# Causal dilated convolution with a gate: first loads in other pieces, a fixed order of issue, and another order of units

## The chip, the cores and the metric

One core of one Trainium2 chip runs the kernel; the arrays lie in the chip's memory before and after. The metric is device time in microseconds (us) of one execution, and the time of a kernel is the median of its runs. The profile is of one execution, recorded by the hardware profiler, and has its own time.

The engines carry the profile's names: PE (TensorE, matmuls), PEld (its weight loads), DVE (VectorE), ACT (ScalarE), POOL (GpSimd) and SP (SyncE, which here issues DMAs only). Each engine works through its own instructions in the order in which they are written down; a semaphore holds an instruction, and all behind it on that engine, until what it needs is done.

## The reference

The input x is 2 x 16000 x 144 (batch, time, channels), the taps w are 15 x 144 x 288, and w_o is 144 x 144, all bf16. Each output row is a causal convolution with dilation 2, a gate and a projection:

```python
dil = 2
pad = (K - 1) * dil
xp = jnp.pad(x, ((0, 0), (pad, 0), (0, 0)))
h = jnp.einsum('btc,cd->btd', xp[:, pad:pad + T, :], w[0])
for i in range(1, K):
    off = pad - i * dil
    h = h + jnp.einsum('btc,cd->btd', xp[:, off:off + T, :], w[i])
f = h[..., :D].copy()
g = h[..., D:].copy()
z = jnp.tanh(f) * _sigmoid(g)
return z @ w_o
```

with D = 144 and K = 15.

## The kernel before

**Layout.** The 32,000 rows are cut into 128 stretches of 250, one for each partition, so one tile is one time step of all stretches: 128 rows by 144 channels. To use time steps as the matmul's stationary operand, each tile is transposed. The 144 channels are split into 128 (tiles XA, multiplied by the taps WA) and 16 (eight steps of 16 channels packed into 128 rows: tiles XB, taps WB). A matmul multiplies a 128x128 tile by 128x288 taps into a PSUM bank of 288 columns: 144 for f, 144 for g. Time is counted in octets of eight tiles; there are 31, and 28 tiles of history precede them.

**The first ten rows and the rest.** The first ten time steps are computed straight, with 15 taps each for the 128 channels and two matmuls for the 16 (`direct`, L1096, `direct_b`, `direct_all`, L1127). The rest goes through a fast scheme that needs fewer matmuls: DVE forms differences of transposed tiles (V, DU, DD, BD, and over pairs of octets GX, GU, GV, GD, lines L724 to L810) and sums of taps (WC, WS, WT, WV, WD, `wsum`, L659). Two octets make a pair and each pair two units, one for its even and one for its odd steps; there are 30 units.

**A unit.** Its steps are named in a string, `ORDER` (L18), which is walked once for each unit; steps that take a bank to the next unit's partial sums act one unit ahead. XC and XR make the part with DU and GU (taps WT and WS, WB with XB), CV and CD the part with XA, V and DD (WT, WV, WD), SR the part with GX (WC), EF the part with GV and the four accumulations by DVE (L1061), DD the last part with GD and BD. UP is POOL's addition (L997), PJ a projection (L918) with its eviction by ACT (L922). Copies of a bank into another (`copy`, L960) and evictions to UC, UD and XS (`evict`, L475 as one piece for adjacent banks, L478 as two) are ACT's. The last part of a unit is evicted by ACT as sigmoid and tanh into TG, and DVE multiplies them into Z (L841). Z is transposed by DMA (ZT) and projected.

**The planner.** `_Graph` holds all operations with their reads and writes. `schedule` runs a simulated list scheduling, ten passes, with costs from the `dur` numbers written at each operation and due times of the pass before, and the best pass gives each engine's order and the PSUM banks. PE may take operations up to `PE_WIN` (L17) places ahead of the program's order; other engines go by due time. The parameter `soft` of `add` makes an operation start after others in the plan without a semaphore on the chip; before the change no operation uses it. `assign` gives each kind of DMA a ring of semaphores, and a load whose turn in the ring falls on a semaphore in use waits until the earlier load has landed.

**The start.** PE first runs 40 warm-up matmuls (`warm`, L583) on constants. The first 38 tiles of x (28 of history, 2 that the octets leave over, and octet 0) come in four pieces (`pro_pieces`: 14, 8, 8 and 8 tiles). Each of the first three comes in two loads, of 112 and of 15 partitions; partition 0 of all three comes by two small loads on ACT's queue, and its place in the history is zeroed later. The taps come in four (`wa_pieces`: 10 to 14, 6 to 9, 2 to 5, 0 and 1). SP issues them in the planner's order: x, x, x, x, WA, WA, x, x, WA, x, WA, then WB (L559), then the first chunks of Xr (`load_xchunk`, L665), the x for later octets, each of 16 tiles. The taps use three semaphores, and the fourth waits for the first one; every chunk of Xr carries a dependence on the load of taps 0 and 1 (`wa_op`), and so do the 16 loads of w_o on POOL's queue. The 15-row piece of the first x load, like the others, is issued by SP.

`transposes` (L600) transposes a piece's tiles by PE (L612) into a PSUM bank that ACT or DVE evicts into XA (L618), and DVE zeroes the columns that lie across the two batches (L625) once for each octet. `compact_pro` packs the last 16 channels (L577), and `b_halo` (L631) zeroes part of that on POOL, has PE transpose it (L647) and ACT evict it to XB (L650). The banks 6 and 7 serve these transposes besides 5, and bank 6 the warm-up (`BANK_O`). Six banks, 0 to 5, hold the first six rows. Then, for each piece of taps, six groups of matmuls (`direct`) run, and the transposes of the next piece stand ahead of the six. Two matmuls (L1119) then clear banks 6 and 7.

**Later octets.** ACT copies the first four octets of Xr to STA (L684) and DVE the later ones; SP transposes STA into XA by DMA (L689). For the 16 channels DVE makes C from Xr (L675), SP transposes T from C (L711), stores T to memory and loads it back (s<-T, XB<-s, L701), and copies part of the last octet's XB (XB<-XB, L701).

## Time and profile before

| | |
|---|---|
| median of the runs | 313.43 us (3 runs, 313.32 to 313.61) |
| the profiled execution | 314.19 us, of which the span is 312.6 us |
| instructions | 7564, of them 2586 matmuls |
| busy share of the span | PE 97%, DVE 93%, ACT 83%, PEld 76%, POOL 32% |
| granted clock of TensorE | full speed in all 40 slices |
| moved by DMA | 48.47 MB, mean 155 GB/s |

The span runs from the first to the last recorded instruction; the execution's own time holds what lies around it as well. Times in the views are us from the start of the span, and durations are of one group of like instructions, in which the end of one may overlap the start of the next. L816 is the line of `region` and `mm`, where most matmuls are recorded, so they are told apart by their tiles.

### The profile page before, as it was taken

The page shows a single profiled execution, that of the slowest core. Times are in us where ns is not written, and L with a number is a line of the kernel's source. Part 1 is how long each engine was busy: PE and PEld are TensorE (multiplying, and loading weights), DVE is VectorE, ACT ScalarE, POOL GpSimd, SP SyncE. Part 2 cuts the span into 40 slices and gives each one's busy share as a digit, 9 for nine tenths or more (in the row PEclk, how much of TensorE's full clock was granted, in tenths as well). Part 3 has the DMA queues.
Part 4 walks back from the last instruction along what each step waited for, and adds up shares of the span by engine and source line. Part 5 has one row for each costly group of instructions (what it writes and reads, how often), then busy time and mean ns, then how long its engine had stood idle before and what let it go on. Part 6 is the DMA issues. An engine that isn't in the chain of part 4 may idle for free.

```text
span 312.6 us, 7564 instructions
## 1 busy us (share of the span) xinstructions
PE 303.5 (97%) x2586; PEld 237.9 (76%) x2586; DVE 291.6 (93%) x651; ACT 258.7 (83%) x835; POOL 99.9 (32%) x89
## 2 busy tenths in 40 slices
PE   7989998999999999999999999999999999999995
PEld 7867675677787878787777778777787877778784
DVE  1899699999999999999999999999999999999764
ACT  3365697788998888899888888998888899888894
POOL 7920142333222333332133333222333332233330
PEclk9999999999999999999999999999999999999999
DMA  7964755859667485856749686674759586461342
GB/s 209 302 110 133 168 138 140 126 159 135 197 154 184 137 177 163 173 168 151 186 130 173 165 173 189 138 203 116 160 164 209 159 116 147 120 142 52 103 115 113
DMA packets 100067, 48.47 MB, mean 155 GB/s; under 512 B 88222, under 2 KB 90719, under 8 KB 100029
## 3 DMA queue, kind: packets, MB, share of 16 engines
q1 hardware_dynamic: 99513, 47.66, 63.3%
q0 software_dynamic: 512, 0.33, 0.5%
q8 instruction: 20, 0.33, 0.5%
q14 instruction: 18, 0.15, 0.1%
q10 hardware_dynamic: 4, 0.01, 0.0%
HBM read 13.77 MB, written 10.20 MB: 77 GB/s over the span
## 4 chain that ended last, share of the span: by engine, by line
PE 89%; DMA 4%; ACT 2%; DVE 2%; SPq 1%; issue 1%; ACTq 0%
PE PS L816 79%; PE PS L918 9%; DMA Xr<-in_x_dram 2%; DMA WA<-in_w_dram 2%; DVE DD L724 1%; ACT PS L960 1%; ACT STA L684 1%; SPq L517 1%; SPq L559 1%; ACT TG L478 1%; PE PS L878 0%; PE PS L940 0%; DVE Xp L987 0%; ACT XA L618 0%; ACT TG L475 0%
## 5 line engine op out<-in xcount | busy, mean ns | idle before, releaser
L997 POOL TENSOR_TENSOR UX<-UC,XS 128x576 f32<-128x576 f32 x60 | 84.3, 1425 | 201.2 <-ACT UC L475 95.5
L816 PE MATMUL PS<-WA,GD 128*128 128x288 bf16 x450 | 87.3, 286 | 1.2 <-DVE PS L1061 1.2
L960 ACT ACTIVATE PS<-PS 128x288 f32<-128x288 f32 x210 | 81.4, 443 | 0.5 <-PE PS L816 0.4
L816 PE MATMUL PS<-WB,BD 128*128 128x288 bf16 x240 | 67.5, 286 | 0.0
L475 ACT ACTIVATE TG<-PS 128x288 bf16<-128x288 f32 x130 | 47.6, 438 | 16.8 <-PE PS L816 16.7
L478 ACT ACTIVATE TG<-PS 128x144 bf16<-128x144 f32 x240 | 50.7, 315 | 8.7 <-PE PS L816 8.6
L816 PEld LDWEIGHTS PS<-WA,GD 128*128 128x128 bf16 x450 | 42.5, 98 | 14.5 <-DVE PS L1061 2.5
L922 ACT ACTIVATE OS<-PS 128x432 bf16<-128x432 f32 (+1 forms) x88 | 43.1, 490 | 12.4 <-PE PS L918 11.9
L1061 DVE TENSOR_TENSOR PS<-PS,Xp 128x288 f32<-128x288 f32 x120 | 49.5, 458 | 1.5 <-PE PS L816 0.5
L1061 DVE TENSOR_TENSOR PS<-PS,UX 128x288 f32<-128x288 f32 x120 | 49.3, 456 | 0.0
L987 DVE TENSOR_TENSOR Xp<-PS,UD 128x576 f32<-128x576 f32 x60 | 42.7, 751 | 3.6 <-ACT UD L478 3.4
L816 PE MATMUL PS<-WS,GU 128*128 128x288 bf16 x210 | 45.0, 286 | 0.4 <-ACT PS L960 0.4
L918 PE MATMUL PS<-WOR,ZT 128*128 128x144 bf16 (+1 forms) x322 | 43.3, 253 | 0.0
L816 PE MATMUL PS<-WC,GV 128*128 128x288 bf16 x210 | 37.7, 287 | 0.5 <-ACT PS L960 0.5
L816 PE MATMUL PS<-WB,XB 128*128 128x288 bf16 x140 | 37.6, 286 | 0.0
L918 PEld LDWEIGHTS PS<-WOR,ZT 128*128 128x128 bf16 x322 | 28.4, 98 | 5.8
L841 DVE TENSOR_TENSOR Z<-TG 128x576 bf16<-128x576 bf16 (+1 forms) x63 | 27.7, 440 | 3.7 <-ACT TG L475 3.6
L816 PE MATMUL PS<-WD,DD 128*128 128x288 bf16 x210 | 30.7, 286 | 0.0
L816 PEld LDWEIGHTS PS<-WB,BD 128*128 128x128 bf16 x240 | 23.5, 98 | 5.9
L816 PEld LDWEIGHTS PS<-WS,GU 128*128 128x128 bf16 x210 | 20.4, 98 | 6.6 <-ACT PS L960 1.3
L816 PEld LDWEIGHTS PS<-WD,DD 128*128 128x128 bf16 x210 | 19.5, 98 | 6.7 <-ACT PS L960 1.7
L816 PE MATMUL PS<-WT,DU 128*128 128x288 bf16 x120 | 24.5, 286 | 0.1
(87 smaller groups left out, 475.0 us busy)
## 6 DMA issues: line engine op xcount, KB each, us to landing
out_dram<-OS SPq DMA_DIRECT2D x31, 288.0 KB, 2.3
Xr<-in_x_dram SPq DMA_DIRECT2D x15, 576.0 KB, 4.6
XB<-XB SPq DMA_DIRECT2D x30, 192.0 KB, 3.2
XB<-s SPq DMA_DIRECT2D x59, 32.0 KB, 2.0
s<-T SPq DMA_DIRECT2D x30, 32.0 KB, 3.5
WA<-in_w_dram SPq DMA_DIRECT2D x2, 288.0 KB, 5.4
ZT<-Z SPq DMA_TRANSPOSE x32, 3.0
Xp<-in_x_dram SPq DMA_DIRECT2D x2, 252.0 KB, 4.9
```

Source lines behind the costliest of these rows:

```text
L475: return e.activation(bass.AP(t[:].tensor, off + (0 if st > 0 else n), [[row, NP], [st, 2], [1, n]]), bass.AP(PS[:].tensor, lo * 512 + c0, ...
L478: ins = e.activation(bass.AP(t[:].tensor, off + i * n, [[row, NP], [1, n]]), bass.AP(PS[:].tensor, q.phys * 512 + c0, [[8 * 512, NP], [1, ...
L517: return e.dma_start(tile_ap, src)
L559: return e.dma_start(WB[0:n * DB, par, :], src)
L816: return lambda t: t.matmul(bank(b), lhsT=lhs(), rhs=rhs(), start=start, stop=True, skip_group_check=True)
L841: g.add("dve", lambda v: v.tensor_tensor(dst(), TG[:, s, 1, 2 * k:2 * k + n, :], TG[:, s, 0, 2 * k:2 * k + n, :], ALU.mult), r=[("TG", s, ...
L918: return t.matmul(PS[:, c0:c0 + n * D], lhsT=ZT[:, zt, blk_, :], rhs=WOR[:, wi_:wi_ + n, :].rearrange("p a b -> p (a b)"), start=first, st ...
L922: g.add("act", lambda e: e.activation(OS[:, os_, a:c, :].rearrange("p e d -> p (e d)"), PS[:, bo.phys * 512:bo.phys * 512 + (c - a) * D], ...
L960: g.add("act", lambda e: e.activation(bank(c), bank(b), ACT.Copy), r=[("bank", b)], w=[("bank", c)], dur=0.29, prio=prio)
L987: return v.tensor_tensor(ue(u % NU, q, 0, 2).rearrange("p (v n) -> p v n", v=2), src, UD[:, u % NUD, :, :], ALU.add)
L997: op = g.add("pool", lambda p: p.tensor_tensor(UX[:, u % NU, h, :, :], UC[:, 0, :, :], bass.AP(XS[:].tensor, h * N2, [[2 * N2, NP], [0, 2] ...
L1061: g.add("dve", lambda e, dst=dst, src=src, ua=ua: e.tensor_tensor(bank(dst), bank(src), ua(), ALU.add), r=[("bank", src), ("UX", us, h) if ...
```

## The change

What it does, part by part:

- The first loads come in five pieces of x (10, 4, 8, 8, 8 tiles) and five of taps (13 and 14, 10 to 12, 6 to 9, 2 to 5, 0 and 1), issued by SP in turn: a piece of x, then a piece of taps. A chain of `soft` links (`first`) fixes this order in the plan, on SP and on ACT. The 15-row load of the first x piece moves to ACT's queue, with the halo rows, ahead of ACT's first activation.
- Semaphores: five for the taps instead of three, twelve for x instead of eight. WB and the first two Xr chunks are linked behind the taps by `soft` alone, and the dependence of chunks on taps 0 and 1 is gone. The loads of w_o keep theirs, and those taps are now issued last.
- The transposes: in the plan 50 warm-up matmuls (40 and 10) stand ahead of the first piece's transposes instead of 40, and the 12 behind them are gone; the transposes of the next piece stand between the second and the third group of `direct` of a piece; `b_halo` stands between the fourth and fifth group of the fourth piece. Octet -3, which two banks hold, is transposed, evicted and zeroed by halves, and taps wait for the half that they read (`xa_key`).
- The warm-up writes bank 4 instead of 6 (`BANK_O`).
- `ORDER` and `PE_WIN` change, and with them the plan of all engines: in the string DD00 moves behind CV, CD0, XC0 and CD1, XR0 ahead of SR0, SR1 ahead of DD11 and DD10, and UP0 and UP1 to the end.

```diff
-PE_WIN = 28
-ORDER = "EF0 PJ EF1 XC1 DD00 CV CD0 XC0 CD1 XR1 DD11 UP0 SR0 XR0 DD01 DD10 PJ UP1 SR1 PJ"
+PE_WIN = 26
+ORDER = "EF0 PJ EF1 XC1 CV CD0 XC0 CD1 DD00 XR1 XR0 SR0 PJ DD01 SR1 PJ DD11 DD10 UP0 UP1"
...
-    BANK_O = 6
+    BANK_O = 4
...
-        wa_pieces = [(10, 15), (6, 10), (2, 6), (0, 2)]
...
-        pro_pieces = [(0, 14), (14, 22), (22, E0), (E0, EP)]
...
+        chain = {"sp": None, "act": None}
+
+        def first(eng, fn, key, dur, dma, nbytes):
+            op = g.add(eng, fn, w=key, dur=dur, dma=dma, nbytes=nbytes, soft=(chain[eng],))
+            chain[eng] = op
+            return op
+
+        def halo(key, e0, n):
+            first("act", lambda e: e.dma_start(flat(Xp[0:1, e0:e0 + n, :]), bass.AP(x_t, 0, [[L * D, 1], [1, n * D]])), [key], 0.5, "xp", n * 288)
         for pi, (e0, e1) in enumerate(pro_pieces):
-            if pi:
...
-                g.add("sp", ld_w(t0, t1), w=[("WA", pi - 1)], dur=0.55, dma="wa", nbytes=(t1 - t0) * 128 * N2 * 2)
             if e0 >= H:
-                g.add("sp", ld_x(flat(Xp[:, e0:e1, :]), 0, NP, e0, e1), w=[("Xp", pi, 0), ("Xp", pi, 1)], dur=0.45, dma="xp", nbytes=NP * (e1 - e0) * D * 2)
-                continue
-            g.add("sp", ld_x(flat(Xp[1:1 + n16, e0:e1, :]), 1, 1 + n16, e0, e1), w=[("Xp", pi, 0)], dur=0.45, dma="xp", nbytes=n16 * (e1 - e0) * D * 2)
-            g.add("sp", ld_x(flat(Xp[1 + n16:NP, e0:e1, :]), 1 + n16, NP, e0, e1), w=[("Xp", pi, 1)], dur=0.45, dma="xp", nbytes=15 * (e1 - e0) * D * 2)
-        g.add("act", lambda e: e.dma_start(flat(Xp[0:1, 0:H, :]), bass.AP(x_t, 0, [[L * D, 1], [1, H * D]])), w=[("Xp", 0, 2)], dur=0.5, dma="xp", nbytes=8064)
-        g.add("act", lambda e: e.dma_start(flat(Xp[0:1, H:E0, :]), bass.AP(x_t, 0, [[L * D, 1], [1, KD * D]])), w=[("Xp", 2, 2)], dur=0.5, dma="xp", nbytes=576)
...
-        wa_op = g.add("sp", ld_w(t0, t1), w=[("WA", 3)], dur=0.55, dma="wa", nbytes=(t1 - t0) * 128 * N2 * 2)
...
+                first("sp", ld_x(flat(Xp[:, e0:e1, :]), 0, NP, e0, e1), [("Xp", pi, 0), ("Xp", pi, 1)], 0.45, "xp", NP * (e1 - e0) * D * 2)
+            else:
+                first("sp", ld_x(flat(Xp[1:1 + n16, e0:e1, :]), 1, 1 + n16, e0, e1), [("Xp", pi, 0)], 0.45, "xp", n16 * (e1 - e0) * D * 2)
+                first("act" if pi == 0 else "sp", ld_x(flat(Xp[1 + n16:NP, e0:e1, :]), 1 + n16, NP, e0, e1), [("Xp", pi, 1)], 0.45, "xp", 15 * (e1 - e0) * D * 2)
+                if pi == 0:
+                    halo(("Xp", 0, 2), 0, H)
+                    halo(("Xp", 3, 2), H, KD)
+            t0, t1 = wa_pieces[pi]
+            wa_op = first("sp", ld_w(t0, t1), [("WA", pi)], 0.5, "wa", (t1 - t0) * 128 * N2 * 2)
+        xp_keys = [[("Xp", pi, 0), ("Xp", pi, 1)] + ([("Xp", 0, 2)] if pi < 4 else []) + ([("Xp", 3, 2)] if pi == 3 else []) for pi in range(5)]
...
+        g.add("act", lambda a: a.activation(SCR[:, 0:32], SCR[:, 32:64], ACT.Sigmoid), r=["SCR"], w=["SCR2"], dur=1.5, soft=(chain["act"],))
...
-        g.add("sp", ld_wb(0), w=[("WB", 0)], dur=0.5, dma="wb", nbytes=73728)
-        g.add("sp", ld_wb(1), w=[("WB", 1)], dur=0.5, dma="wb", nbytes=64512)
+        first("sp", ld_wb(0), [("WB", 0)], 0.5, "wb", 73728)
+        first("sp", ld_wb(1), [("WB", 1)], 0.5, "wb", 64512)
...
             for o in range(-4, 1):
-                es = [e for e in range(max(0, E0 + 8 * o), E0 + 8 * o + 8)]
-                if not (e0 <= es[0] < e1):
-                    continue
                 for h, (j0, j1) in enumerate(XA_PARTS[o]):
                     eng, b = XA_ENG[o][h]
+                    es = [E0 + 8 * o + j for j in range(j0, j1)]
+                    if not e0 <= es[0] < e1:
+                        continue
                     fns = []
                     for e in es:
                         i = oct_of(e)[1]
-                        if j0 <= i < j1:
-                            fns.append((lambda e_, b_, i_: (lambda t: t.transpose(PSb[:, b_ * 1024 + 128 * i_:b_ * 1024 + 128 * i_ + 128], Xp[:, e_, 0:DA], ID[:])))(e, b, i))
+                        fns.append((lambda e_, b_, i_: (lambda t: t.transpose(PSb[:, b_ * 1024 + 128 * i_:b_ * 1024 + 128 * i_ + 128], Xp[:, e_, 0:DA], ID[:])))(e, b, i))
...
-                    g.add(eng, ev, r=[("bank", HB[b])], w=[("XA", aslot(o), h)] if o < 0 else [("XA", aslot(o))], dur=(0.08 + 0.115 * (j1 - j0)) if eng == "act" else (0.05 + 0.08 * (j1 - j0)))
-                z0 = 2 if o == -4 else 0
-                z1 = 6 if o == -1 else 8
-                if o < 0:
-                    def zc(v, o_=o, i0_=z0, i1_=z1):
-                        dst = XA[:, aslot(o_), i0_:i1_, :].rearrange("p s (b q) -> p s b q", q=SEG)[:, :, :, 0]
-                        return v.memset(dst, 0.0)
-                    g.add("dve", zc, r=[("XA", aslot(o), h) for h in range(len(XA_PARTS[o]))], w=[("XA", aslot(o))], dur=0.08)
+                    last = h == len(XA_PARTS[o]) - 1
+                    key = ("XA", aslot(o)) if last else ("XA", aslot(o), h)
+                    g.add(eng, ev, r=[("bank", HB[b])], w=[key], dur=(0.08 + 0.115 * (j1 - j0)) if eng == "act" else (0.05 + 0.08 * (j1 - j0)))
+                    z1 = min(j1, 6) if o == -1 else j1
+                    if o < 0 and j0 < z1:
+                        def zc(v, o_=o, i0_=j0, i1_=z1):
+                            dst = XA[:, aslot(o_), i0_:i1_, :].rearrange("p s (b q) -> p s b q", q=SEG)[:, :, :, 0]
+                            return v.memset(dst, 0.0)
+                        g.add("dve", zc, r=[("XA", aslot(o), q) for q in range(h)] if last else [], w=[key], dur=0.08)
...
-            return g.add("sp", ld_x(flat(Xr[:, s, 0:c - a, :]), 0, NP, E0 + a, E0 + c), w=[("Xr", s)], dur=0.5, dma="xr", nbytes=NP * (c - a) * D * 2)
+            return g.add("sp", ld_x(flat(Xr[:, s, 0:c - a, :]), 0, NP, E0 + a, E0 + c), w=[("Xr", s)], dur=0.5, dma="xr", nbytes=NP * (c - a) * D * 2, soft=(chain["sp"],) if ci < 2 else ())
...
+        def xa_key(e):
+            o, i = oct_of(e)
+            return ("XA", aslot(o), 0) if o == -3 and i < XA_PARTS[o][0][1] else ("XA", aslot(o))
...
-                  r=[("XA", aslot(o)) for o in sorted(set(oct_of(e - DIL * i)[0] for i in range(t0, t1)))] + [("WA", pi)], w=[("bank", b)], dur=(t1 - t0) * MM)
+                  r=sorted(set(xa_key(e - DIL * i) for i in range(t0, t1))) + [("WA", pi)], w=[("bank", b)], dur=(t1 - t0) * MM)
...
-        load_xchunk(0).deps.add(wa_op)
+        load_xchunk(0)
+        transposes(0)
+        warm(10)
         for pi, (t0, t1) in enumerate(wa_pieces):
-            if pi == 0:
-                transposes(0)
-                warm(12)
-            if pi < 3:
-                transposes(pi + 1)
-            if pi == 2:
-                b_halo()
             for k in range(6):
+                if k == 2 and pi < 4:
+                    transposes(pi + 1)
+                if k == 4 and pi == 3:
+                    b_halo()
                 direct(k, HB[k], pi, t0, t1)
...
-                load_xchunk(nl[0]).deps.add(wa_op)
+                load_xchunk(nl[0])
...
-        g.assign(mksem, {"xp": 8, "wa": 3, "wb": 2, "xr": NX, "xa": 4, "xb": 10, "zt": 3, "st": 4, "wor": 16})
+        g.assign(mksem, {"xp": 12, "wa": 5, "wb": 2, "xr": NX, "xa": 4, "xb": 10, "zt": 3, "st": 4, "wor": 16})
```

17 lines of the change are left out of this document (7 added, 10 removed).

## The prediction

> **What bounds the kernel now.** I read the page first, then the busy time by stretches, then the order of time where an engine idles.
>
> ```profile
> span 312.6 us, 7564 instructions
> ...
> PE 89%; DMA 4%; ACT 2%; DVE 2%; SPq 1%; issue 1%; ACTq 0%
> ...
> XB<-XB SPq DMA_DIRECT2D x30, 192.0 KB, 3.2
> ```
>
> The span is 312.6 us, in an execution that took 314.19, so 1.59 us lie around it. The median of the runs shown is 313.43, 0.76 below the profiled execution; I work out a difference from the profile and take it off the median. TensorE (PE) carries 89% of the chain that ended last. One copy XB<-XB goes with each octet (x30), so there are 15 pairs of octets, 14 of them after 57 us.
>
> ```profile
> 0.00:10.00 10.00, 8.11 (x91) 7.54 (x92) 3.18 (x14) 4.12 (x8) 7.75 (x14) 1.00 0.86 231
> 10.00:20.00 10.00, 8.80 (x88) 7.13 (x86) 9.03 (x26) 5.47 (x9) 7.85 (x16) 1.00 0.67 194
> ...
> 60.00:280.00 220.00, 220.00 (x1851) 172.74 (x1850) 218.53 (x483) 196.31 (x652) 66.64 (x49) 1.00 0.68 160
> ```
>
> From 60 to 280 us PE is never idle, VectorE (DVE) idles 220 - 218.53 = 1.47 us and ScalarE (ACT) is busy 196.31, 89%: both stand close behind. Matmuls overlap in this view, so a short wait of PE shows only in their starts:
>
> ```profile
> 127.78 0.41 PE L816 MATMUL PS<-WC,GX 128*128 128x288 bf16 x2
> ...
> 129.62 0.53 PE L816 MATMUL PS<-WC,GV 128*128 128x288 bf16 x3
> 129.99 0.29 PE L816 MATMUL PS<-WA,GV 128*128 128x288 bf16 x1
> 130.23 0.42 PE L816 MATMUL PS<-WC,GV 128*128 128x288 bf16 x2
> ```
>
> A 128x288 matmul follows the one before it after 0.122 us (worked out below), but from 129.99 to 130.23 it is 0.24: 0.12 us lost in this pair, and 14 x 0.12 = 1.7 us in all pairs if each is like it. What else PE can save lies before 57 us and behind 305.
>
> ```profile
> 1.68 4.13 PE L583 MATMUL PS<-ONES,ID 128*128 128x128 bf16 x40 [1.68 <-POOL ID L562]
> ...
> 5.65 0.94 PE L612 MATMUL PS<-ID,Xp 128*128 128x128 bf16 x14
> 6.19 1.02 DVE L618 COPY XA<-PS 128x768 bf16<-128x768 bf16 x2 [5.21 <-PE PS L612]
> ...
> 6.80 0.84 PE L583 MATMUL PS<-ONES,ID 128*128 128x128 bf16 x12 [0.21 <-DVE XA L618]
> 6.86 0.07 DVE L625 MEMSET XA<- 128x12 bf16 x1
> ...
> 7.75 0.30 DVE L659 TENSOR_TENSOR WC<-WA 128x288 bf16<-128x288 bf16 x1
> ...
> 7.93 3.84 PE L816 MATMUL PS<-WA,XA 128*128 128x288 bf16 x30
> ...
> 15.86 1.67 ACT L684 ACTIVATE STA<-Xr 128x512 bf16<-128x512 bf16 x3 [2.58 <-DMA Xr<-in_x_dram]
> ...
> 17.44 1.00 ACT L618 ACTIVATE XA<-PS 128x1024 bf16<-128x1024 bf16 x1
> ...
> 18.49 0.62 PE L647 MATMUL PS<-ID,XS 128*128 128x128 bf16 x8 [1.20 <-ACT XA L618]
> ...
> 21.89 0.41 PE L1119 MATMUL PS<-WB,ID 128*128 128x288 bf16 x2
> ```
>
> In this view the columns are start, duration, engine, line, operation, count, and in brackets the idle time before it with what ended it. Forty warm-up matmuls run until the first transposes start at 5.65; 12 more fill PE from 6.80, 8 tiles are transposed, and the taps start at 7.93. From there to 21.89 PE stands still once, 1.20 us before 18.49: the 8 transposes into bank 6 wait for ACT's eviction of 17.44, which stands in ACT's queue behind three copies that waited 2.58 us for the first chunk of Xr.
>
> ```profile
> 0.82 0.41 SPq L517
> 1.29 0.47 SPq L517
> ...
> 2.65 4.70 DMA WA<-in_w_dram
> ...
> 9.50 6.34 DMA Xr<-in_x_dram
> ```
>
> In the chain of waits these are SP's first two issues, the first taps (360 KB) and that chunk. The chunk left SP only at 9.50, because the last tap load ahead of it waited for a semaphore that the first taps still held, and took 6.34 us.
>
> **The change, part by part.** Lengths: a 128x288 matmul steps (3.84 - 0.286) / 29 = 0.1225 us (the row of 30 at 7.93; 0.286 is one alone, as the 0.29 at 129.99), a warm-up matmul or a transpose (0.84 - 0.22) / 11 = 0.056.
>
> *Start of the taps.* Ten warm-up matmuls now stand ahead of the first transposes, so these start at 5.65 + 10 x 0.056 = 6.21. Ten transposes and then four end at 6.21 + 14 x 0.056 = 6.99. DVE's eviction follows the first transpose by 6.19 - 5.65 = 0.54, its zeroing by another 6.86 - 6.19 = 0.67, then come 0.07 and some 0.05 for the semaphore: the first tap starts at 7.54, 0.39 earlier. But 22 tiles were transposed by 7.93 and now 14 by 7.54; the other 8 cost 8 x 0.056 = 0.45 later. Net +0.06: the smaller first piece buys nothing, because the warm-up block ends later than x lands:
>
> ```profile
> Xp<-in_x_dram SPq DMA_DIRECT2D x1, 441.0 KB, 4.3
> ...
> Xp<-in_x_dram SPq DMA_DIRECT2D x1, 59.1 KB, 4.0
> ```
>
> 441 KB landed at 0.82 + 4.3 = 5.1 and the 59 KB issued behind them at 1.29 + 4.0 = 5.3, so transfers land in order; 1.14 MB were through at 2.65 + 4.70 = 7.35 (three pieces of x and the first taps), or 0.31 MB/us after the first. The second x piece ends 0.65 MB into the new order, at some 5.8, before its transposes. Bounds: -0.5 if the earlier x lets the warm-up end earlier too, +0.5 if that piece comes after 7.
>
> *Taps in five pieces, transposes between the second and third tile of a piece.* From the first tap to the clearing matmuls (21.89) PE has 90 matmuls, 24 transposes of x and 12 of the second operand: 7.54 + 90 x 0.1225 + 36 x 0.056 = 20.58 if nothing waits. That is 1.31 earlier: the 1.20 wait and its restart go. Three covers are needed. (a) DVE's zeroing of half an octet, which the third tile's taps need, stands behind a sum over the first two tap pieces. These end 0.87 MB into the queue, at about 6.5; DVE's evictions end at 7.8, the sum (0.30, row of 7.75) and the zeroing at 8.2, and PE has 8 matmuls to do until 7.54 + 0.98 = 8.52. (b) The last octet is transposed 62 taps and 24 transposes after 7.54, at 16.5, and evicted 1.00 later. (c) PE asks for it 12 matmuls and 4 transposes on, at 18.2, so ACT's copies of Xr (1.67) must start by 15.5. The chunk is issued sixteenth, at 0.82 + 15 x 0.47 = 7.9 instead of 9.50. By the shapes 3.16 MB lie in the queue up to its end; 2.31 are through by 10.0 (231 GB/s), and the rest takes 4.4 us at 194 GB/s: 14.4. If it lands at 15.86 again, PE waits 0.3. GpSimd's (POOL's) w_o loads now wait for the last taps and so stay out of its way longer; nothing reads them before 38 us. I take -1.3, bounds -1.36 and -0.9.
>
> *Xr chunks issued right behind the loads* give cover (c); behind them SP holds only transposes that wait for them.
>
> *What follows, 32 to 57 us.* Here DVE sets the pace:
>
> ```profile
> 30.19 0.55 SPq L701 DMA_DIRECT2D XB<-XB  x1
> 30.78 1.25 SPq L711 DMA_TRANSPOSE T<-C  x1
> ...
> 33.73 0.69 DVE L724 TENSOR_TENSOR BD<-XB 128x1024 bf16<-128x1024 bf16 x1
> ...
> 35.57 1.55 DVE L987 TENSOR_TENSOR Xp<-PS,UD 128x576 f32<-128x576 f32 x2 [1.16 <-ACT UD L478]
> ```
>
> and of the copy at 30.19, the tile's own view says:
>
> ```profile
> DMA to landing us min/median/max: 2.5/2.5/2.5
> ```
>
> DVE's long run starts at 35.57, ended by an ACT eviction that PE feeds, so it moves with PE if its inputs do. The difference at 33.73 (BD) stands ahead of it in DVE's queue and needs the copy XB<-XB, the end of a chain on SP that starts with DVE's copy of the first Xr chunk. That chunk lands 1.4 earlier, but DVE, busy 9.03 of the 10 us from 10 to 20, now has two more sums ahead of the copy: I let 0.3 through. And one transpose T (1.25) now precedes the XB copy on SP: 30.19 - 0.3 + 1.25 = 31.1. Landed 2.5 us later (this copy) or 3.2 (the median of its kind, above) it is 33.6 or 34.3, BD takes 0.6, and the run would start at 35.57 - 1.30 = 34.27. Cost 0 to 0.65; I take 0.2, nearer to this copy's own row.
>
> ```profile
> 36.44 0.30 PE L816 MATMUL PS<-WS,GU 128*128 128x288 bf16 x1 [0.43 <-ACT PS L960]
> ...
> 48.77 0.42 PE L816 MATMUL PS<-WA,GD 128*128 128x288 bf16 x2 [0.72 <-DVE PS L1061]
> ```
>
> The 0.43 at 36.44 goes, as the matmuls that feed its copy now precede the eight of WD; but DVE's run bounds what follows: 0, bounds 0 and -0.4. At 48.77 PE waits 0.72 for DVE's accumulation. DVE's new order puts both 128x576 additions ahead of the four accumulations instead of one, so this wait grows by what the next one loses: 0, bounds +/-0.6.
>
> *The body.* PE's work is the same but for two warm-up matmuls. The new unit order reaches it changed little: in one pair six matmuls of WS,GU follow each other before GX. This row pair's GX ends 3 x 0.1225 = 0.37 later, at 128.56, and its copy on ACT starts only at 128.98, since ACT is busy with UC:
>
> ```profile
> 128.40 0.72 ACT L478 ACTIVATE UC<-PS 128x288 f32<-128x288 f32 x2
> 128.98 0.45 ACT L960 ACTIVATE PS<-PS 128x288 f32<-128x288 f32 x1
> ...
> 129.76 0.41 ACT L960 ACTIVATE PS<-PS 128x288 f32<-128x288 f32 x1
> ```
>
> So 0.42 us cover it, and without them PE loses what is missing at 129.62. The order on ACT up to the copy at 129.76 stays, so the 0.12 per pair stays too. 0; bounds -1.7 and +2.8 (below).
>
> *The tail.* Three output matmuls, half as wide as the others and so under 3 x 0.1225 = 0.37 us, now stand before the last two groups of GD, and their eviction before ACT's last two gates:
>
> ```profile
> 306.15 0.85 ACT L478 ACTIVATE TG<-PS 128x144 bf16<-128x144 f32 x4
> ...
> 307.33 0.30 DVE L841 TENSOR_TENSOR Xr<-TG 128x288 bf16<-128x288 bf16 x1
> ```
>
> The last gate ends near 307.35 instead of 306.15 + 0.85 = 307.0; but DVE multiplied only at 307.33, behind other work. +0.1, bounds 0 and +0.4.
>
> The sum: -1.3 (with the +0.06 of the start in it) + 0.2 + 0 + 0 + 0.1 = -1.0 us; 314.19 becomes 313.2, and the median 313.43 - 1.0 = 312.4.
>
> **The rivals.**
>
> *More is won.* The waits of 0.43 and 0.72 go, and 0.01 of the 0.12 in each pair: another 0.43 + 0.72 + 0.14 = 1.3 us, 311.1. For it: the new order puts the matmuls that feed ACT's copy and DVE's accumulation further ahead of those that wait for them. Against: DVE's run starts no earlier for it, and the queue of ACT's evictions stays.
>
> *The gain is eaten by DVE.* The XB copy lands at 34.3, which costs 0.65 instead of 0.2, and the wait at 48.77 grows by half of a 128x576 addition (1.55 / 4 = 0.4): -1.0 + 0.45 + 0.4 = -0.15, 313.3. For it: SP's chain moves only 0.3. Against: BD waited for no DMA here.
>
> *Smaller pieces land later.* The chunk of (c) must be there by 15.5. If three more transfers ahead of it each hold up the queue for one issue of SP (0.47, the row of 1.29), it lands at 14.4 + 1.4 = 15.8, with ACT's copies PE waits 0.3, and the 0.3 of SP's chain to the XB copy is lost: -1.0 + 0.3 + 0.3 = -0.4, 313.0. For it: the transfers in flight fill the DMA engines (0.86 busy in the first 10 us). Against: 59 KB landed only 0.2 us behind 441 KB, so a piece costs little.
>
> The Trainium skill (DMA: Bandwidth & Descriptors, Rules for kernel authors) wants transfers of 1 MiB and more and calls those under 64 KB mostly overhead; from its table of sizes (64 KB in 0.95 us, 1 MB in 6.15) I estimate 0.6 us for each transfer. By that rule the chunk lands at 16.2 and the sum is 0; by the row of the 59 KB it is -1.0, and no run so far shows the rule here.
>
> *Slower: the body loses at ACT.* At 129.76 the copy that frees 130.23 is late already, with no cover. If the new order lets ACT reach it 0.2 us later, PE loses 14 x 0.2 = 2.8: 313.43 - 1.0 + 2.8 = 315.2; from 0.07 us per pair on it outweighs the start. For it: ACT is 89% busy and has one queue for all its evictions. Against: the order between UC and that copy is the same.
>
> **How the numbers follow.** Forecast 0.53 (its own range 311.9 to 312.9), more won 0.17, eaten by DVE 0.08, smaller pieces 0.06, slower body 0.16. The time is 312.4. The range takes in the case of 311.1 below and those of 313.0 and 313.3 above, with a little beside them, and leaves out the slower body: 310.9 to 313.6. Faster or slower by 0.2% (0.63 us, about what a measurement of this kernel can tell from no change) means below 312.8 or above 314.06. Faster: 0.50 of the forecast and 0.17, 0.67. Slower 0.16. Within: 0.17.
>
> **What would show it.** Right: first transposes near 6.2, first taps near 7.5, clearing matmuls near 20.6 with no wait above 0.3 before them; the first Xr chunk landed before 15; DVE's long run from 34.4; and the 0.12 us after the copy of 129.76 as before. Wrong: taps that start after 8, a wait of PE between 8 and 18 for DVE's zeroing or a tap load, an XB copy that lands after 34, new waits of PE for ACT between 60 and 280, or a last gate that ends after DVE's other work is done.

## The result and the profile after

| kernel | median of the runs | ratio to before, 95% interval |
|---|---|---|
| before, beside it | 313.38 us (12 runs, 312.6 to 313.76) | |
| the changed kernel | 314.68 us (12 runs, 313.78 to 315.76) | 1.0046 [1.0032, 1.0061] |

The change made the kernel 1.3 us slower where 1.0 us faster was forecast, and the time lies outside the forecast range. Three executions of the runs below stand far apart from the others of their kernel (328.52 us in a3, 453.97 in c2, 1807.2 in c4); the medians hold them, the ratios and intervals don't. The page of the changed kernel, of an execution that took 314.31 us:

```profile
span 312.6 us, 7557 instructions
...
PEclk9999999999999999999999999999999999999999
...
PE 84%; DVE 10%; issue 2%; SPq 1%; DMA 1%; ACT 1%; POOL 0%; DVEq 0%; ACTq 0%; POOLq 0%
```

DVE's share of the chain that ended last grew from 2 to 10%, so somewhere PE now waits for DVE; how much can't be read off this share, for in a second profile of the same kernel (a1 below) it is 3%. The order of time of PE at the start (columns as in the prediction):

```profile
1.68 4.52 PE L590 MATMUL PS<-ONES,ID 128*128 128x128 bf16 x50 [1.68 <-POOL XS L571]
6.04 0.94 PE L618 MATMUL PS<-ID,Xp 128*128 128x128 bf16 x14
7.37 2.38 PE L823 MATMUL PS<-WA,XA 128*128 128x288 bf16 x18 [0.39 <-DVE XA L632]
...
18.00 0.61 PE L654 MATMUL PS<-ID,XS 128*128 128x128 bf16 x8
18.45 2.12 PE L823 MATMUL PS<-WA,XA 128*128 128x288 bf16 x16
20.41 0.41 PE L1129 MATMUL PS<-WB,ID 128*128 128x288 bf16 x2
```

This is the forecast start: first taps at 7.37 (7.54), clearing matmuls at 20.41 (20.58), no wait before 18.45. So the loss lies behind it, or before's start was not what its profile showed. Before was therefore profiled again (run a2 below, an execution of 313.40 us):

```profile
1.68 4.45 PE L583 MATMUL PS<-ONES,ID 128*128 128x128 bf16 x40 [1.68 <-POOL ID L562]
5.92 1.64 PE L612 MATMUL PS<-ID,Xp 128*128 128x128 bf16 x14
...
8.55 3.84 PE L816 MATMUL PS<-WA,XA 128*128 128x288 bf16 x30
...
17.75 0.61 PE L647 MATMUL PS<-ID,XS 128*128 128x128 bf16 x8
18.20 3.10 PE L816 MATMUL PS<-WA,XA 128*128 128x288 bf16 x24
21.14 0.41 PE L1119 MATMUL PS<-WB,ID 128*128 128x288 bf16 x2
```

The wait of 1.20 us on which the forecast rested is not there: the 8 transposes start at 17.75 without one (the first Xr chunk landed at 14.48, not 15.84), and the clearing matmuls stand at 21.14, not 21.89. The taps, on the other hand, start 0.62 later than in before's first profile, since 14 transposes took 1.64 us instead of 0.94. Two profiles of one kernel differ by 0.62 us in the first taps and by 1.20 us in this wait, in opposite directions, so all later comparisons use a2 and several profiles of the new start.

DVE, in the order of time, in the changed kernel and then in a2:

```profile
33.70 0.69 DVE L731 TENSOR_TENSOR BD<-XB 128x1024 bf16<-128x1024 bf16 x1 [1.37 <-DMA XB<-XB]
34.31 0.75 DVE L994 TENSOR_TENSOR Xp<-PS,UD 128x576 f32<-128x576 f32 x1
...
38.06 1.54 DVE L731 TENSOR_TENSOR DU<-XA 128x512 bf16<-128x512 bf16 x1
39.52 0.82 DVE L1068 TENSOR_TENSOR PS<-PS,UX 128x288 f32<-128x288 f32 x2
40.26 0.68 DVE L805 TENSOR_TENSOR GU<-DU 128x1024 bf16<-128x1024 bf16 x1
...
45.15 1.90 DVE L817 TENSOR_TENSOR GV<-V 128x1024 bf16<-128x1024 bf16 x1
46.97 1.53 DVE L994 TENSOR_TENSOR Xp<-PS,UD 128x576 f32<-128x576 f32 x2
```

```profile
32.97 0.69 DVE L724 TENSOR_TENSOR BD<-XB 128x1024 bf16<-128x1024 bf16 x1
34.82 1.55 DVE L987 TENSOR_TENSOR Xp<-PS,UD 128x576 f32<-128x576 f32 x2 [1.16 <-ACT UD L478]
...
38.68 0.43 DVE L724 TENSOR_TENSOR DU<-XA 128x512 bf16<-128x512 bf16 x1
39.77 1.16 DVE L798 TENSOR_TENSOR GU<-DU 128x1024 bf16<-128x1024 bf16 x1
...
44.88 1.89 DVE L724 TENSOR_TENSOR DD<-V 128x1024 bf16<-128x1024 bf16 x1
46.70 0.74 DVE L987 TENSOR_TENSOR Xp<-PS,UD 128x576 f32<-128x576 f32 x1
```

DVE's long run, named by its first 128x576 addition, starts at 34.31 instead of 34.82, so 0.51 earlier. In front of it DVE now waits 1.37 us for the copy XB<-XB, where before it waited for ACT. Behind it DU takes 1.54 us instead of 0.43, and the second pair of 128x576 additions comes as one block (1.53) behind GV. Ahead of that pair one instruction takes 1.9 us in both kernels, GV in the changed one and DD in a2. PE's waits for DVE's accumulations in the same stretch, in the changed kernel and then in a2:

```profile
40.03 0.42 PE L823 MATMUL PS<-WA,GD 128*128 128x288 bf16 x2 [0.78 <-DVE PS L1068]
48.94 0.30 PE L823 MATMUL PS<-WA,GD 128*128 128x288 bf16 x1 [1.44 <-DVE PS L1068]
...
50.39 0.42 PE L823 MATMUL PS<-WA,GD 128*128 128x288 bf16 x2
```

```profile
48.00 0.42 PE L816 MATMUL PS<-WA,GD 128*128 128x288 bf16 x2 [0.71 <-DVE PS L1061]
...
49.39 0.42 PE L816 MATMUL PS<-WA,GD 128*128 128x288 bf16 x2 [0.48 <-DVE PS L1061]
```

The wait of 0.78 us at 40.03 is new. The one at 48 grew by 0.73, but the next one, 0.48 in a2, is gone.

From 60 to 290 us no loss was added: the matmul that follows the late copy still loses its 0.11 us in each pair (129.78 to 130.01 less 0.122).

```profile
129.78 0.29 PE L823 MATMUL PS<-WA,GV 128*128 128x288 bf16 x1
130.01 0.66 PE L823 MATMUL PS<-WC,GV 128*128 128x288 bf16 x4
```

### The profile page after: what moved, and what is told of

It reads as the page before. It is cut to its first block, busy times and chain, and to the rows that moved or that the text cites. A ratio compares the mean times of both kernels' runs of the same rounds, so it can differ in the third digit from the quotient of the medians.

```text
span 312.6 us, 7557 instructions
## 1 busy us (share of the span) xinstructions
PE 303.3 (97%) x2584; PEld 238.1 (76%) x2584; DVE 292.0 (93%) x652; ACT 259.3 (83%) x828; POOL 100.5 (32%) x89
## 4 chain that ended last, share of the span: by engine, by line
PE 84%; DVE 10%; issue 2%; SPq 1%; DMA 1%; ACT 1%; POOL 0%; DVEq 0%; ACTq 0%; POOLq 0%
PE PS L823 73%; PE PS L925 9%; PE PS L590 1%; DVE V L731 1%; DVE DD L731 1%; DVE DU L731 1%; DMA XB<-XB 1%; DVE Xp L994 1%; DVE PS L1068 1%; SPq L718 1%; DVE WC L666 1%; SPq L708 1%; DVE WD L666 0%; DVE GV L817 0%; DVE BD L731 0%
## 5 line engine op out<-in xcount | busy, mean ns | idle before, releaser
L967 ACT ACTIVATE PS<-PS 128x288 f32<-128x288 f32 x210 | 79.6, 434 | 2.0 <-PE PS L823 1.4
L475 ACT ACTIVATE TG<-PS 128x288 bf16<-128x288 f32 x140 | 50.7, 436 | 15.7 <-PE PS L823 15.6
L478 ACT ACTIVATE TG<-PS 128x144 bf16<-128x144 f32 x220 | 47.0, 312 | 9.8 <-PE PS L823 9.6
L823 PE MATMUL PS<-WS,GU 128*128 128x288 bf16 x210 | 44.1, 286 | 0.5 <-ACT PS L967 0.5
```

The costliest lines, as they stand in the source:

```text
L475: return e.activation(bass.AP(t[:].tensor, off + (0 if st > 0 else n), [[row, NP], [st, 2], [1, n]]), bass.AP(PS[:].tensor, lo * 512 + c0, ...
L478: ins = e.activation(bass.AP(t[:].tensor, off + i * n, [[row, NP], [1, n]]), bass.AP(PS[:].tensor, q.phys * 512 + c0, [[8 * 512, NP], [1, ...
L823: return lambda t: t.matmul(bank(b), lhsT=lhs(), rhs=rhs(), start=start, stop=True, skip_group_check=True)
L967: g.add("act", lambda e: e.activation(bank(c), bank(b), ACT.Copy), r=[("bank", b)], w=[("bank", c)], dur=0.29, prio=prio)
```

## A table that splits every kernel in three

From each profile three numbers are read: where DVE's long run starts, when the last matmul starts (308.88 in the changed kernel), and the execution's time. They split it into the start (up to DVE's run), the body (from there to the last matmul) and the rest (behind it). All in us; "XB" is the landing of the copy XB<-XB of about 33.

| kernel | first tap | clearing | XB | DVE's run | body | rest | execution |
|---|---|---|---|---|---|---|---|
| before (first profile) | 7.93 | 21.89 | 32.67 | 35.57 | 273.52 | 5.10 | 314.19 |
| a2: before again | 8.55 | 21.14 | 32.05 | 34.82 | 273.49 | 5.09 | 313.40 |
| c1: before, two moves | 8.44 | 21.20 | 31.69 | 34.88 | 273.41 | 5.11 | 313.40 |
| b2: old start, changed orders | 8.55 | 21.14 | 33.86 | 34.70 | 274.55 | 5.16 | 314.41 |
| changed kernel | 7.37 | 20.41 | 33.68 | 34.31 | 274.57 | 5.43 | 314.31 |
| a1: changed kernel again | 8.48 | 21.52 | 34.66 | 35.30 | 274.66 | 5.41 | 315.37 |
| b4: changed, 31 warm-ups | 6.64 | 19.97 | 32.67 | 33.53 | 274.54 | 5.42 | 313.49 |
| b3: changed, DU later | 7.73 | 20.77 | 33.97 | 34.61 | 274.10 | 5.42 | 314.13 |
| c4: changed, two moves | 7.06 | 20.11 | 33.31 | 33.94 | 272.90 | 5.43 | 312.27 |
| d3: c4 with 31 warm-ups | 6.64 | 19.85 | 33.30 | 33.94 | 272.86 | 5.44 | 312.24 |
| e2: d3, chain earlier | 6.64 | 19.79 | 30.87 | 33.35 | 272.78 | 5.42 | 311.55 |
| b1: new start, before's orders | 7.97 | 21.02 | 33.16 | 35.01 | 273.58 | 5.45 | 314.04 |
| c2: b1, fewer semaphores | 7.42 | 20.47 | 33.13 | 34.99 | 273.57 | 5.47 | 314.03 |
| c3: b1, 31 warm-ups, moves | 6.11 | 19.20 | 31.59 | 33.44 | 273.41 | 5.47 | 312.32 |
| d1: b1, ZT behind XB<-s | 8.30 | 21.34 | 33.97 | 35.84 | 273.77 | 5.46 | 315.07 |
| d2: b1, 15 rows on SP | 7.85 | 20.90 | 33.36 | 35.22 | 273.64 | 5.43 | 314.29 |
| d4: b1, w_o earlier | 8.08 | 21.13 | 33.41 | 35.27 | 273.63 | 5.44 | 314.34 |
| e1: b1, C copy earlier | 8.23 | 21.28 | 33.14 | 34.99 | 273.56 | 5.44 | 313.99 |

Body and rest repeat within 0.2 and 0.1 us for like orders and like starts; in the two kernels that were profiled twice, it is the start that varies. So the sum can be read off: against a2 the changed kernel has a body 1.08 longer (1.17 in a1), a rest 0.34 longer (0.32), and a start between 0.51 earlier and 0.48 later. 1.08 + 0.34 and about nothing for the start is 1.4 us; the medians differ by 1.3. One profile is one execution, though: those of c4 (312.27, median 313.66) and b4 (313.49, median 314.39) lie far below the median of their kernel, so from them body and rest are taken, and not the time.

## The experiments

In all of them the ratio is to before, timed on the same chip.

**Both kernels again (a1, a2).** No edit.

> The changed kernel once more, for a second profile and more times. Theory start: the clearing matmuls come 1.4 us earlier (20.4) in every execution, and the gain is given back between 30 and 58 us, where a DVE instruction of 0.42 us took 1.54 beside POOL's addition; the time is 313.6 to 314.7 and its spread comes from that stretch. Theory body: executions slower than the profiled one lose in the pairs from 60 to 290 us, so a profile with a span over 313 shows PE waits there that sum to 0.5 us or more above the first profile's.

> The kernel before once more, for a second profile: its first profile (314.19 us) lies 0.8 above the median of its runs. Theory start: the second profile lies nearer to 313.4 and is shorter between 30 and 58 us, by the 0.7 to 1.2 us that a DVE instruction beside POOL's addition loses there. Theory body: it is shorter somewhere between 60 and 290 us.

a1: 315.16 us, ratio 1.0059 [1.0047, 1.0071], above what was expected; a2: 313.41 us, 1.0005 [0.9996, 1.0014]. In a1 the start shows what varies:

```profile
1.68 5.51 PE L590 MATMUL PS<-ONES,ID 128*128 128x128 bf16 x50 [1.68 <-POOL ID L569]
6.99 1.10 PE L618 MATMUL PS<-ID,Xp 128*128 128x128 bf16 x14
8.48 0.79 PE L823 MATMUL PS<-WA,XA 128*128 128x288 bf16 x5 [0.38 <-DVE XA L632]
```

Fifty warm-up matmuls take 5.51 us here and 4.52 above. Single starts in the trace step 107 ns up to a moment (4.86 us in the changed kernel's profile, 7.20 in a1) and 56 ns after it.

**The parts alone, as the planner makes them (a3, a4).** a3 is the changed kernel with the old unit order, a4 before with the new one:

```diff
-PE_WIN = 26
-ORDER = "EF0 PJ EF1 XC1 CV CD0 XC0 CD1 DD00 XR1 XR0 SR0 PJ DD01 SR1 PJ DD11 DD10 UP0 UP1"
+PE_WIN = 28
+ORDER = "EF0 PJ EF1 XC1 DD00 CV CD0 XC0 CD1 XR1 DD11 UP0 SR0 XR0 DD01 DD10 PJ UP1 SR1 PJ"
```

> The new loads and transposes with the old order of units and the old window of PE. Theory start: the clearing matmuls at 20.4 as with the whole change, and the time hangs on 30 to 58 us: 312.0 to 313.6, faster than the change by 1 us if its new order of units is what costs. Theory body: the planner makes another body of it too (ACT has 863 instructions instead of 839 and 833, more evictions in two halves), and by ACT's longer queue the pairs get longer: 315 to 319.

> The old loads and transposes with the new order of units and the new window of PE. Theory start: the clearing matmuls stay at 21.9; nothing is gained at the start and the rest is as in the change: 314.5 to 315.5. Theory body: the planner's body for this pairing is another again (ACT 845 instructions), and the time goes with it: 314 to 318.

a3: 324.49 us, 1.0351 [1.0334, 1.0367]; a4: 327.61 us, 1.0458 [1.044, 1.0476]. Both fall far outside what was expected, and neither tells a part's price: the planner makes another plan for each pairing (ACT has 858 and 841 recorded instructions, in before 835), with large losses in single stretches of the body. In a4 PE waits 3.04 us for DVE at 106.59, and its 128x288 matmuls then step 0.24 us instead of 0.12 until 109.7, at a granted clock of 0.50. An edit of the string is no way to undo a part. From here the planner's lists are written out, as numbers of operations for each engine and PSUM bank, and replayed, so that one instruction can be moved alone:

```diff
-        _ms = g.schedule()
+        _ms = g.replay(PLAN, SEATS)
```

**The parts alone, with orders written out (b1, b2).** b1 has the new start and, from about 27 us on, before's orders on every engine; b2 the old start and the changed kernel's orders from there.

> The new loads and transposes with the orders of the kernel before on every engine from some 27 us on (orders and banks written out, not planned). Theory stretch: the change loses 1.4 us between 30 and 60 us by its order of units there, and its start is worth between -0.4 and +0.5 according to when PE's matmuls get fast; then this kernel is at 313.0 to 313.8, level with before, and its PE loses about 4.0 us between 20 and 60 as before does, not 5.4. Theory start: the start itself is what costs (50 slow warm-up matmuls); then it stays at 314.5 to 315.2.

> The old loads and transposes with the changed kernel's orders on every engine from some 28 us on (written out, not planned). Theory stretch: 1.0 to 1.5 us above before, 314.4 to 314.9, with PE losing about 5.4 us between 20 and 60. Theory start: level with before, 313.4.

b1: 314.12 us, 1.0029 [1.0018, 1.004]; b2: 314.40 us, 1.0032 [1.002, 1.0043]. Each costs some 0.9 to 1.0 us, and their sum is about the change (1.0046 and 1.0059). The table says where: b2 has the long body (274.55) and before's rest (5.16), b1 before's body (273.58) and the long rest (5.45). That the start alone loses was the surprise: b1 lies between what its two theories gave.

**What lengthens the body (b3, c4, c1).** DU starts at 38.06 while POOL adds UX, and so does GV at 45.15; each is held until POOL's addition is done (the last section has the rows). b3 moves DU (291) behind two more accumulations, c4 also the DD of the fourth octet (292), which stands ahead of GV, behind both 128x576 additions and the accumulations, so that GV slides ahead of POOL's next addition. c1 tries the like in before: DD (277) behind the accumulations, and the second 128x576 addition (331) right behind the first. The diff shows b3's move and c4's together.

```diff
-    "dve": [... 310, 291, 302, 303, 295, ... 289, 292, 296, ... 412, 361, 297, ...
+    "dve": [... 310, 302, 303, 291, 295, ... 289, 296, ... 412, 361, 292, 297, ...
```

> The changed kernel's own orders written out, with one DVE instruction moved: the difference DU that took 1.54 us at 38.06 stands two accumulations later. Theory port: it waits for POOL's second addition, and PE's wait of 0.94 behind it goes to about 0.3; 0.5 to 0.7 us faster than the changed kernel (314.0 to 314.6). Rival: the accumulations wait for POOL's addition themselves, and nothing is won (315).

> The changed kernel, its orders written out, with DU later as in b3 and the difference DD of octet 4 behind the accumulations. Theory port: beside the 0.5 us of b3 another 0.8 to 1.2 of the 1.6 that PE waits at 47 goes: 312.8 to 313.3, about level with before or below. Rival: as for c1, 313.9 as b3.

> The kernel before, its orders written out, with two DVE instructions moved: the difference DD of octet 4, which took 1.90 us at 45.64 beside POOL's addition instead of 0.68, stands behind the eight accumulations, and both 128x576 additions stand ahead of them. Theory port: DVE loses 1.2 us there to POOL and PE waits 0.9 + 0.65 for it; with the move these two waits sum to 0.6 or less, and the kernel is 0.8 to 1.2 us faster than before (312.1 to 312.5). Rival: POOL's addition, not DVE, sets the accumulations, the wait only moves and the time stays at 313.3.

b3: 313.86 us, 1.0021 [1.0005, 1.0037], body 274.10, 0.47 shorter than the changed kernel's. Counted from DVE's run, its matmuls come 0.81 us earlier by the wait at 48 (48.43 - 34.61 against 48.94 - 34.31); 0.34 of that go again between 85 and 87 us, where the changed kernel, with the same order of matmuls, loses nothing. c4: 313.66 us, 1.0001 [0.9988, 1.0015], body 272.90, 1.67 shorter than the changed kernel's and 0.6 shorter than before's; its median stayed above what was expected. Moving two instructions of DVE takes back more than the body lost. The two don't count alike: the wait behind DU is new with the change, and in b3 none is left there, while the 1.9 us ahead of the 128x576 additions stand in before too, so the second move wins something that the change had not lost. In c4's order of time DU is held a shorter time and GV not at all:

```profile
38.49 0.81 DVE L798 TENSOR_TENSOR DU<-XA 128x512 bf16<-128x512 bf16 x1
...
43.37 0.69 DVE L884 TENSOR_TENSOR GV<-V 128x1024 bf16<-128x1024 bf16 x1
44.45 1.55 DVE L1061 TENSOR_TENSOR Xp<-PS,UD 128x576 f32<-128x576 f32 x2 [0.40 <-PE PS L890]
```

c1 is a miss: 313.27 us, 0.9992 [0.9981, 1.0003], body 273.41. There too the long DVE instruction of 44.88 is gone and PE's wait at 48 falls, but three waits for DVE come in its place, 0.20 us at 49.74, 0.38 at 56.77 and 0.25 at 57.81, none of which stands in a2 (the 0.49 for ACT at 55.97 does, at 56.90). DVE itself comes no further: it now idles 0.39 and 0.41 us on the way and starts GD at 51.77, in a2 at 51.80. c4 meets one such wait, 0.55 us at 56.54, and keeps the rest of its gain; why before's order keeps nothing was not tried further.

**The start: warm-up (b4).** 31 warm-up matmuls instead of 50.

```diff
-        warm(40)
+        warm(30)
...
-        warm(10)
+        warm(1)
```

> The changed kernel's own orders written out, with 31 warm-up matmuls instead of 50. Theory pace: matmuls take 107 ns for 128 columns until a moment between 3.2 and 5.6 us after the first, whatever their number, so 19 fewer let the first transposes start when x has landed (5.5 to 5.8) instead of 6.0 to 7.0: the first taps at 6.9 to 7.4, and 0.3 to 1.1 us faster than the changed kernel, with less spread. Rival count: the pace needs the matmuls, PE stays slow longer, and the taps start no earlier.

b4: 314.39 us, 1.0028 [1.0012, 1.0044], 0.3 us below the changed kernel's median, with intervals that overlap. The profile has first taps at 6.64 and DVE's run at 33.53, 0.8 before the earlier of the changed kernel's two profiles.

```profile
1.68 3.49 PE L657 MATMUL PS<-ONES,ID 128*128 128x128 bf16 x31 [1.68 <-POOL ID L636]
```

31 take 3.49 us, (3.49 - 0.22) / 30 = 0.109 each: all of them at the slow step.

**The start: what else is in b1's loss (c2, c3, d1, d2, d4).** c2 is b1 with before's number of semaphores, c3 adds 31 warm-ups and c1's two moves, d1 puts ZT<-Z (257) behind two loads XB<-s on SP, d2 moves the 15-row load back from ACT's queue to SP's, d4 issues four w_o loads (197, 207, 196, 198) earlier on POOL's, and the w_o loads depend on the third piece of taps there, not on the last.

```diff
-        g.assign(mksem, {"xp": 12, "wa": 5,
+        g.assign(mksem, {"xp": 8, "wa": 3,
...
-    "sp": [... 270, 257, 143, 145, 152, ...
+    "sp": [... 270, 143, 145, 257, 152, ...
...
-                first("act" if pi == 0 else "sp", ld_x(flat(Xp[1 + n16:NP, e0:e1, :]), 1 + n16, NP, e0, e1), [("Xp", pi, 1)], 0.45, "xp", 15 * (e1 - e0) * D * 2)
+                first("sp", ld_x(flat(Xp[1 + n16:NP, e0:e1, :]), 1 + n16, NP, e0, e1), [("Xp", pi, 1)], 0.45, "xp", 15 * (e1 - e0) * D * 2)
...
-    "pool": [18, 20, 19, 21, 23, 22, 74, 75, 76, 197, 207, 196, 198, ...
+    "pool": [18, 20, 19, 21, 23, 22, 197, 207, 196, 198, 74, 75, 76, ...
...
-                op.deps.add(wa_op)
+                op.deps.add(wa_ops[2])
```

> The new start with the old body (b1, 0.29% above before) with 8 semaphores for x and 3 for the taps as before instead of 12 and 5. Theory semaphores: the six more cost 0.17 us outside the span (1.73 to 1.77 against 1.5 to 1.6) and 0.1 at its end; this kernel is 0.2 to 0.3 faster than b1 (313.8). Rival: these differences come from elsewhere, and it stays at 314.1 with 1.7 us outside the span.

> The new start with 31 warm-up matmuls and the old number of semaphores, with the old body and its two DVE moves. If the theories pace, stretch, port and semaphores all hold their sums add: clearing matmuls at 19.9 to 20.6, 0.5 to 1.0 us earlier than with 50 warm-ups, of which DVE lets half through, and 0.8 to 1.2 from the moves: 312.0 to 312.8. If DVE lets nothing of the earlier start through: 313.0.

> The new start with the old body (b1) with one DMA moved on SP: the transpose of Z stands behind the first two loads XB<-s, as in the kernel before, instead of ahead of them. Theory XB chain: in b1 the copy XB<-XB was issued at 30.66 and landed at 33.1, 1.1 us later than before, and PE's wait for it (0.3 in b1, 0.83 in c2) eats what the start gains; with the move it is issued 0.6 to 1.2 us earlier and the kernel is 0.3 to 0.6 us faster than b1 (313.5 to 313.8). Rival: s<-T lands late anyway, because the w_o loads run beside it, and the copy moves less than 0.3: 314.1.

> The new start with the old body (b1) with the load of 15 rows of the first x piece back on SP. Theory queue: the 0.17 us more outside the span (1.73 against 1.55) and the 0.15 more behind the last matmul (3.7 against 3.55) of every kernel with the new start come from that load on ACT's queue; they go, and the time falls by 0.3 to 313.8, though the first taps move up to 0.3 later. Rival: they come from something else of the start, stay, and the time is 314.1 to 314.4.

> The new start with the old body (b1), with four of the sixteen loads of w_o ahead of POOL's work for XB and hung on the third piece of taps instead of the last, as in the kernel before. Theory w_o: the loads end 1.5 to 2 us earlier (by 20 instead of 22), s<-T and the XB copies behind them land 0.5 to 0.9 earlier, and the time falls by 0.2 to 0.5 (313.6 to 313.9). Rival: the four loads delay the first chunk of Xr and with it the last transposes instead: 314.1 to 314.5.

c2: 314.06 us, 1.0025 [1.0013, 1.0037], rest 5.47. c3: 312.73 us, 0.9984 [0.9969, 0.9998]. d1: 314.70 us, 1.004 [1.0027, 1.0053], a miss: the two loads XB<-s that it let pass landed earlier (28.85 and 29.18, in b1 30.39 and 30.65), but the copy XB<-XB that it was to free didn't (33.98, in b1 33.16). d2: 314.29 us, 1.003 [1.0017, 1.0043], rest 5.43. d4: 313.90 us, 1.0012 [1.0, 1.0024], though its one profile (of an execution of 314.34 us) shows no gain in the start. The rest stays at 5.4 with fewer semaphores and with the 15 rows on SP, so neither alone is its cause. What does bind in these kernels is the copy XB<-XB: in b1, c2, d1, d2 and d4 DVE's run starts 1.85 to 1.87 us after it lands.

**The chain to XB<-XB (d3, e1, e2).** d3 is c4 with 31 warm-ups. The chain begins with DVE's copy C<-Xr (139), goes over T, s, XB and ends in XB<-XB. e1 is b1 with that copy ahead of one DU (184) and a sum; e2 is d3 with the same, and with the second T<-C (222) behind XB<-XB on SP, as in before.

```diff
-    "dve": [... 175, 174, 184, 176, 139, 181, ...
+    "dve": [... 175, 174, 139, 184, 176, 181, ...
...
-    "sp": [... 153, 214, 222, 151, 212, ...
+    "sp": [... 153, 214, 151, 222, 212, ...
```

> The changed kernel with the two DVE moves of c4 (313.66) and 31 warm-up matmuls instead of 50. Theory pace: the first taps 0.4 to 1.2 us earlier, of which the XB copy lets half through: 312.9 to 313.3. Rival: nothing comes through, 313.7.

> New start with before's orders, and one instruction moved: DVE's copy C<-Xr stands one place ahead of the DU of octet -1 and the two weight sums behind it, 0.56 us earlier by the profile of the new start with old body (15.51 instead of 16.07; Xr had landed at 14.73). Theory (the new start's loss is the chain of transfers C, T, s, XB, copy XB<-XB, which begins with this copy): the copy XB<-XB lands 0.4 to 0.6 us earlier counted from the first tap, PE's waits for it near 33 to 36 us go, and the ratio to before falls from 1.0029 to 1.0010 to 1.0018 (313.6 to 313.9 us). Rival (the loss is in the rest around the span and at the end): the copy lands earlier, but the ratio stays at 1.0025 to 1.0035.

> The changed kernel with 31 warm-up matmuls and the two moves on DVE (312.77 us, 0.9979), and now also the copy C<-Xr one octet's DU and two sums earlier, and on SP the second T<-C behind the copy XB<-XB, as in before. Theory of the chain: the copy XB<-XB is issued 1.2 us earlier by the T moved and 0.3 to 0.5 us by the copy C; where it bounds the body, the time falls by 0.3 to 0.6 us, to 312.2 to 312.5 (0.996 to 0.9972). Rival (with the moved DD and DU the chain no longer sets PE's pace): the same as without the moves, 312.6 to 312.9 (0.9975 to 0.9985).

d3: 312.77 us, 0.9979 [0.9968, 0.9989]. e1: 313.99 us, 1.0017 [1.0008, 1.0026], within what the chain's theory gave, though the interval overlaps b1's; but counted from the first tap the copy landed only 0.28 us earlier (33.14 - 8.23 against 33.16 - 7.97), half of the 0.55 that C gained (15.78 - 8.23 against 16.07 - 7.97). A later step of the chain came later (s landed at 26.83, in b1 at 26.12). e2: 311.65 us (5 runs, 311.53 to 312.37), 0.9952 [0.9938, 0.9966], better than the chain's theory gave and the fastest of all; c3 and d3 are the only others whose whole interval lies below 1. DVE in d3 and then in e2:

```profile
33.33 0.69 DVE L798 TENSOR_TENSOR BD<-XB 128x1024 bf16<-128x1024 bf16 x1 [1.55 <-DMA XB<-XB]
33.94 0.75 DVE L1061 TENSOR_TENSOR Xp<-PS,UD 128x576 f32<-128x576 f32 x1
```

```profile
31.62 0.68 DVE L798 TENSOR_TENSOR BD<-XB 128x1024 bf16<-128x1024 bf16 x1
33.35 0.76 DVE L1061 TENSOR_TENSOR Xp<-PS,UD 128x576 f32<-128x576 f32 x1 [1.04 <-ACT UD L545]
```

The copy lands 2.43 us earlier, DVE's run starts 0.59 earlier and now waits for ACT, as in before. So in d3, the changed kernel with 31 warm-ups and two moves, this DMA chain held the run; in the changed kernel itself the same wait stands ahead of BD (1.37 us).

## Why the prediction was wrong, step by step

The forecast was -1.1 us for the start (-1.3 and 0.2), 0 for the stretch from 32 to 57 us and for the body behind it, and +0.1 for the tail. Against a2 the runs show -0.51 and +0.48 for the start, +1.08 and +1.17 for both stretches together, and +0.34 and +0.32 for the rest.

- **Clearing matmuls and Xr chunk: right in the profile, wrong as a gain.** Taps at 7.37 (7.54 forecast), clearing at 20.41 (20.58), the chunk landed at 14.69 (14.4). The -1.3 fell through on its other side: "That is 1.31 earlier: the 1.20 wait and its restart go" took a wait of one execution for the kernel's. The medians stood 0.76 below that execution, and the prediction carried the difference over instead of asking which row it was. a2 answers it: 34.82 for DVE's run, 0.75 earlier than 35.57.
- **"Ten warm-up matmuls ... 5.65 + 10 x 0.056": mis-sized.** That price holds behind the moment when the step changes from 107 to 56 ns. In a1 the moment came late, the transposes started at 6.99 and the taps at 8.48, no earlier than in a2. b4's profile, with 31 in all, has first taps at 6.64, so the ten were not needed there.
- **The XB copy and DVE's run: right against its own baseline.** Landing at 33.68 (33.6 forecast), the run at 34.31 (34.27 and 0.2 of cost). But "BD waited for no DMA here", which spoke against the rival, no longer held: 1.37 us of wait stand there, and e2 wins 0.59 by taking such a wait out of d3. From a2's 32.05 the landing went back by 1.6 us.
- **"What follows, 32 to 57 us", put at 0: the step that failed most.** The body grew by 1.08 us, and neither execution takes this back. "This wait grows by what the next one loses: 0, bounds +/-0.6" was right for the wait it names: it grew from 0.71 to 1.44, and the 0.48 of the next one went. What has no term is the wait of 0.78 at 40.03: a DVE difference can fall beside one of POOL's additions, and in the new order DU does, ahead of the accumulations that PE needs. b3, which moves DU alone, has no wait there and is 0.81 us ahead by 48 us, of which 0.47 are left in its body. What makes up the remaining loss was not told apart; one more new wait for DVE, 0.17 us, stands at 58.58.
- **The 0.43 at 36.44 goes: half right, and worth nothing, as said.** From 35.74 to 36.22 the matmuls still lose 0.36 us of starts, in a2 (34.98 to 35.69) 0.59.
- **The body per pair: right.** 0.11 us per pair before and after; the rival that slows ACT in each pair fell. The slower side came from a few us near 40 instead.
- **w_o "out of its way": doubtful.** Four of these loads issued earlier gave 1.0012 instead of 1.0029; the intervals just overlap.
- **Smaller pieces land later: not shown.** The chunk landed between 14.1 and 15.7 us in the profiles of the new start, with the old loads between 14.5 and 15.8; no PE wait before the clearing followed from it.
- **The tail, +0.1: nearly right**, 0.15 from the last matmul to the span's end (3.70 against 3.55 in a2). Another 0.2 lie around the span (1.73 against 1.54), and the prediction has no term for it. What causes the 0.34 of the rest is open: semaphores alone and the 15-row load alone are not it, and the other parts of the new start were not tried one by one. Nor does it hang on the new start alone, for a4, with the old start and another plan, has a rest of 5.61 (327.00 less 321.39).

## What to carry to other kernels

When a forecast rests on one wait, look for it in a second execution, and ask first why the profiled one stands off the median. Choose one instruction that the rest of the kernel follows at a fixed distance, and split every run at it: a body that repeats within 0.2 us shows what an order costs even where the start varies by 1 us. And when a reordering moves DVE's work on two SBUF operands, lay POOL's instructions beside it.
